# Gated mix of attention and bilinear FFN: scores delayed to share row-tiled stretches, gate folded into FFN and attention values

## Chip, cores and metric

One core of one Trainium2 chip. Times are device microseconds of an execution; the runs with a profile also give the span from the first to the last instruction. A ratio is the mean time of one kernel's runs over that of the other's of the same rounds, so not quite the ratio of the medians quoted. "Same" means within 2%.

Names in the profile lines: PE is TensorE's matmuls, PEld its weight loads, DVE is VectorE, ACT ScalarE, POOL GpSimd; SP only issues transfers here, and SPq is its queue. A line in order of time reads: start in us, length in us, engine, line of the kernel, operation, written tile <- read tiles, count, and in brackets the idle time before it and what ended that.

## The reference

```python
# B=1, S=2048, D=512, 32 heads of 16, F=1376, all bf16
g = sigmoid((x * gate_w).sum(-1, keepdims=True))      # one value per token
q, k, v = heads(x @ wqkv)
a = concat(softmax(q @ k.T / 4) @ v) @ wo
b = ((x @ w_gate) * (x @ w_up)) @ w_down
out = g * a + (1 - g) * b
```

## The kernel before

Queries go in 4 chunks of 512, heads in 4 blocks of 8. A score tile is 128 keys x 512 queries of one head; there are 2048. Scores use row tiling (contraction of 16, padded to 32 rows), almost everything else column tiling (four 32-column matmuls side by side). PSUM is full: psS has two slots of 3 and 2 banks for scores that ACT exponentiates, psO one bank for the attention sums, psX two banks that serve the projections, the FFN and those scores whose exponential DVE approximates. Four such DVE tiles are one *entry*.

No engine decides anything at run time. A Python program in the kernel plays the engines through with assumed durations and so fixes each engine's order of instructions; semaphores then make the real engines wait in that order.

```python
    def dma(self, eng, fn, deps=(), stream=None, dur=0.5, lat=2.2):   # a landing is reckoned at 2.2 us
        return self.op(eng, fn, deps, stream, 16, dur, lat)
# ... cut ...
            def drain(un, last):              # u half of the FFN: plain copy out of PSUM
                        ev_u[n] = un.free = P.op(
                            "dve", lambda v: v.tensor_copy(usb[0:w, n % 2, :], un.bank[0:w, :]), deps, **EV)
# ... cut: down projection, one bank, multiplied with (1 - g) on the way out
                    ev_b[t] = un.free = P.op("dve",
                        lambda v: v.tensor_scalar(bsb[:, t % 5, :], un.bank, omg[:, t : t + 1], None, ALU.mult), ...)
# ... cut: output projection, another bank, combined: out = g * bank + bsb
                o_comb[t] = b_use[t] = P.op("dve",
                    lambda v: v.scalar_tensor_tensor(
                        dst, bank, gval[:, t : t + 1], bsb[:, t % 5, :], ALU.mult, ALU.add), ...)
# ... cut: Q tiles of a head block reach their padded rows by eight transfers issued by SP
                            o = P.dma("sp", lambda e, r0=r0, p=p: e.dma_start(
                                    QX[r0 : r0 + 16, p, b, :], Qst[r0 : r0 + 16, s, :]), ...)
# ... cut: the order of the fills
        fl.append((20, mk_gate(20)))          # the gate, at position 20 (of 512)
        for b in range(1, NB):
            n0 = 32 * b
            fl.append((n0 - 14, mk_q(b, 0, n0 - 14)))      # Q of block 1 at position 18
```

The softmax here doesn't subtract the row's maximum and nothing guards it: scores larger than these inputs give would overflow.

## Time and profile before

| | before |
|---|---|
| time, median of the runs beside the change | 772.52 us (768.78 to 776.87) |
| profiled span | 765.2 us |
| ACT busy | 97% |
| score tiles on ACT / on DVE | 1624 / 424 (106 entries) |
| mean granted TensorE clock | 0.985 |

The last row is read so: the records know only full and half clock, so 2 x (1 - 0.985) x 765 = 23 us were at half. The lines stand in the prediction. Stretch columns are length, then busy us and (count) of PE, PEld, DVE, ACT, POOL, then granted clock, DMA share, GB/s.

### The profile page before, as it was taken

How to read it: one execution, taken by the hardware profiler on the slowest of the kernel's cores; microseconds unless marked ns; L12 is line 12 of the kernel's file. 1: busy time of each engine (PE TensorE's matmuls, PEld its weight loads, DVE VectorE, ACT ScalarE, POOL GpSimd, SP SyncE). 2: the span in 40 equal slices, each digit the busy share in tenths (PEclk: the TensorE clock that was granted, in tenths of full speed). 3: DMA queues.
4: the chain of work that ended last, by engine and by line, in shares of the span. 5: the costliest groups of instructions: out<-in, count | busy, mean ns of one | idle time of the engine just before them, and what ended most of it. 6: DMA issues, size and time to landing. Idle time of an engine off the chain costs nothing.

```text
span 765.2 us, 20615 instructions
## 1 busy us (share of the span) xinstructions
PE 716.2 (94%) x8934; PEld 216.6 (28%) x8934; DVE 665.0 (87%) x1084; ACT 740.9 (97%) x656; POOL 65.6 (9%) x73
## 2 busy tenths in 40 slices
PE   9997899999999999899999989899999999999987
PEld 3332222222222222222222222222232222222234
DVE  3339999899998789999989799989879899999795
ACT  6999999999999999999999999999999999999994
POOL 8940000000000000000000000000000000000000
PEclk9999999999999999989999999989999999999999
DMA  8900000000000100001001000100001101010000
GB/s 169 284 16 10 20 10 24 16 24 16 9 23 9 45 23 9 23 8 31 9 23 36 16 24 9 29 10 6 26 9 30 37 9 30 2 30 9 22 22 34
DMA packets 32880, 22.80 MB, mean 30 GB/s; under 512 B 20468, under 2 KB 27572, under 8 KB 32788
## 3 DMA queue, kind: packets, MB, share of 16 engines
q1 hardware_dynamic: 31476, 20.42, 10.2%
q8 instruction: 70, 1.15, 0.6%
q0 software_dynamic: 256, 0.79, 0.5%
q10 hardware_dynamic: 1056, 0.26, 0.2%
q14 instruction: 22, 0.18, 0.1%
HBM read 11.24 MB, written 2.35 MB: 18 GB/s over the span
## 4 chain that ended last, share of the span: by engine, by line
PE 41%; ACT 33%; DVE 18%; issue 6%; SPq 1%; DMA 1%; DVEq 0%; ACTq 0%
ACT PT L1423 33%; PE psX L368 14%; PE psS L854 12%; PE psO L1069 11%; DVE SC L997 7%; DVE SC L970 5%; PE psX L950 2%; DVE wk L970 2%; PE psO L1079 1%; SPq L1129 1%; DVE usb L630 1%; PE psX L1079 1%; DMA den<-oraw 1%; DVE hT L643 1%; DVE oraw L1122 1%
## 5 line engine op out<-in xcount | busy, mean ns | idle before, releaser
L1423 ACT ACTIVATE PT<-psS 128x1536 bf16<-128x1536 f32 (+1 forms) x646 | 733.2, 1361 | 7.8 <-PE psS L854 3.8
L854 PE MATMUL psS<-QX,KT 32*128 32x512 bf16 x1624 | 256.4, 388 | 32.4 <-ACT PT L1423 29.9
L970 DVE TENSOR_SCALAR SC<-psX 128x512 int16<-128x512 f32 x304 | 203.8, 683 | 22.8 <-PE psX L950 22.4
L997 DVE TENSOR_SCALAR SC<-SC 128x2048 int16<-128x2048 int16 x304 | 205.4, 694 | 2.5 <-PE psO L1069 0.2
L950 PE MATMUL psX<-QX,KT 32*128 32x512 bf16 x424 | 159.6, 386 | 1.6 <-DVE SC L970 0.8
L1069 PE MATMUL psO<-PT,VV 128*32 128x512 bf16 x1566 | 147.1, 390 | 0.7 <-DVE oraw L1122 0.7
L854 PEld LDWEIGHTS psS<-QX,KT 32*128 32x128 bf16 x1624 | 62.2, 91 | 281.7 <-ACT PT L1423 233.0
L1069 PE MATMUL psO<-SC,VD 128*32 128x512 bf16 x1108 | 104.0, 387 | 4.1 <-DVE SC L997 3.3
L970 DVE TENSOR_SCALAR wk<-psX 128x512 int16<-128x512 f32 x120 | 80.7, 683 | 11.8 <-PE psX L950 11.8
L1182 POOL TENSOR_TENSOR OT<-onum,rb 128x512 bf16<-128x512 f32 x16 | 21.7, 1356 | 680.2 <-DMA rb<-rscr 680.2
L997 DVE TENSOR_SCALAR SC<-wk 128x2048 int16<-128x2048 int16 x90 | 62.8, 717 | 0.6
L1069 PEld LDWEIGHTS psO<-PT,VV 128*32 128x32 bf16 x1566 | 37.8, 95 | 64.5 <-issue 55.8
L368 PE MATMUL psX<-wd,hT 128*32 128x512 bf16 (+1 forms) x704 | 52.6, 381 | 0.2 <-DVE wk L970 0.2
L368 PE MATMUL psX<-xT,wu 128*32 128x512 bf16 x688 | 52.0, 394 | 0.2 <-DVE SC L970 0.2
L368 PE MATMUL psX<-xT,wg 128*32 128x512 bf16 x688 | 50.9, 388 | 0.3 <-DVE wk L970 0.3
L950 PEld LDWEIGHTS psX<-QX,KT 32*128 32x128 bf16 x424 | 37.6, 91 | 21.3 <-DVE SC L970 6.0
L1069 PE MATMUL psO<-SC,VV 128*32 128x512 bf16 x408 | 41.2, 390 | 1.6 <-DVE oraw L1122 1.5
L1069 PEld LDWEIGHTS psO<-SC,VD 128*32 128x32 bf16 x1108 | 27.3, 95 | 47.8 <-DVE SC L997 22.2
L643 DVE TENSOR_TENSOR hT<-psX,usb 128x512 bf16<-128x512 f32 (+1 forms) x44 | 30.1, 684 | 4.0 <-PE psX L368 4.0
L630 DVE CAST usb<-psX 128x512 bf16<-128x512 f32 (+1 forms) x44 | 30.1, 683 | 3.9 <-PE psX L368 3.7
L368 PEld LDWEIGHTS psX<-xT,wu 128*32 128x32 bf16 x688 | 15.2, 97 | 23.0 <-issue 10.3
L368 PEld LDWEIGHTS psX<-xT,wg 128*32 128x32 bf16 x688 | 15.3, 95 | 22.0 <-issue 9.4
(108 smaller groups left out, 351.8 us busy)
## 6 DMA issues: line engine op xcount, KB each, us to landing
rb<-rscr SPq DMA_DIRECT2D x16, 256.0 KB
onum<-oraw SPq DMA_DIRECT2D x124, 32.0 KB, 2.0
QX<-Qst SPq DMA_DIRECT2D x120, 16.0 KB, 1.8
out_dram<-ost SPq DMA_DIRECT2D x12, 128.0 KB, 1.7
wu<-in_B_w_up_dram SPq DMA_DIRECT2D x1, 1376.0 KB, 7.3
wg<-in_B_w_gate_dram SPq DMA_DIRECT2D x1, 1376.0 KB, 10.1
wd<-in_B_w_down_dram SPq DMA_DIRECT2D x1, 1280.0 KB, 12.7
SC<-in_A_x_dram SPq DMA_DIRECT2D x4, 128.0 KB, 3.5
```

The costliest lines, as they stand in the source:

```text
L368: r = pe.matmul(dst_[j : j + 32, :], lhs[:, j : j + 32], rhs, start=s0, stop=s1, tile_position=(0, j), skip_group_check=True,)
L630: "dve", lambda v: v.tensor_copy(usb[0:w, n % 2, :], un.bank[0:w, :]), deps, **EV
L643: lambda v: v.tensor_tensor(hT[0:w, f, :], un.bank[0:w, :], usb[0:w, n % 2, :], ALU.mult),
L854: q = pe.matmul(bank_ap(sl, k_), KT[32 * j : 32 * j + 32, b, kt * 128 : (kt + 1) * 128], QX[32 * j : 32 * j + 32, p, b, :], start=True, st ...
L950: lambda pe: pe.matmul(bank, KT[32 * j : 32 * j + 32, b, kt * 128 : (kt + 1) * 128], QX[32 * j : 32 * j + 32, p, b, :], start=True, stop=True,
L970: lambda v: v.tensor_scalar(i2b(nb)[:, j, :], bank, _LO, _HI, ALU.max, ALU.min),
L997: lambda v: v.tensor_scalar(dstt, src, 0.5, _BASE + _OFF[k], ALU.mult, ALU.add),
L1069: r = pe.matmul(psO[r_, :], vcol(m, kt, k_, j), pj, start=first, stop=last, tile_position=(0, 32 * j), skip_group_check=True)
L1079: r = pe.matmul(psO[r_, 256 * hf : 256 * hf + 256] if w < 2 else psD[r_, 0:256], vcol(m, kt, k_, j, hf) if w < 2 else ones[:, k_, 16 - 16 ...
L1122: o_ev[m] = P.op("dve", lambda v: v.tensor_copy(oraw[:, s, :], psO[:]), deps, **EV)
L1182: lambda g: g.tensor_tensor(OT[:, c % 2, b, :], onum[:], rb[:], ALU.mult),
L1423: lambda a: a.activation(cell_ap(cells[0], n).rearrange("p a b -> p (a b)"), bank_ap(sl, 0, n), ACT.Exp, scale=_LN2 / _OCT,),
```

## The change

Its intent: hand TensorE fewer changes of tiling mode (scores wait so that both slots fall into one row-tiled stretch) and DVE less evacuation. The factor 1-g goes into the u half of the FFN, g into the reciprocal that normalizes attention. Then down and output projection can add up in one bank and leave by one plain copy, for chunks 0 to 2. For that the gate is needed in two other layouts: as a row along tokens for all partitions (omgB), and laid out as the softmax sums are (gC). They are made by a trip through HBM. The FFN's work also gets fixed places, chunk by chunk (the list FFN).

```diff
-    D_IDLE = 0.9
-    SLK = 0.15
+    D_IDLE = 1.5
+    SLK = 0.2
+    STAY = 0.25
-    FFN_FROM, FFN_TO = 60.0, 490.0
+    FFN = [(64, 160, 164, 5), (184, 270, 275, 5), (295, 385, 395, 4), (412, 478, 480, 5)]
+    gsc = nc.dram_tensor("gscr", [2, S], F32, kind="Internal").ap()
 ... gate: values to HBM, turned from [token in tile, tile] to token order
+                        for i, src_ in enumerate([gval, omg]):
+                            o = P.dma("sp", lambda e, i=i, src_=src_: e.dma_start(
+                                    gsc[i].rearrange("(t p) -> p t", p=128), src_[:], allow_slow_non_contiguous=True),
+                                [ogate["g"]], "dgs", lat=4.0)
+                        for i in range(8):                      # back, as gC
+                            o1 = P.dma("sp", ... gC[32 * j : 32 * j + 32, :, 16 * p : 16 * p + 16], ... , [o], "dgc")
+                        ogate["c"] = o1
+                        ld_omg(0, [o])                          # back, as omgB, chunk 0; later chunks likewise
 ... FFN
-                            "dve", lambda v: v.tensor_copy(usb[0:w, n % 2, :], un.bank[0:w, :]), deps, **EV
+                            lambda v: v.tensor_tensor(usb[0:w, n % 2, :], un.bank[0:w, :], omgB[0:w, :], ALU.mult),
 ... attention
+                        lambda v: v.tensor_tensor(rec[:, s, 0:w_], rec[:, s, 0:w_], gC[:, c, 0:w_], ALU.mult),
 ... down and output projection in one bank (mk_dw for mk_d and mk_wo, chunks 0 to 2)
+            return Unit(due, chain(FT + NB, mm), deps, drain)
-        fl.append((20, mk_gate(20)))
+        fl.append((16, mk_gate(16)))
 ... TensorE's order
+                hold = t + cost + 0.6 <= need_s() - SLK        # was: cost + 0.49, and for fills only
+            if s and P.mode == "s" and t < s_ready <= t + STAY:  # stay row-tiled, put a DVE score in between
 ... cut: column values picked by pressure, bookkeeping
```

More of the change, by code (lines that the diff above doesn't have):

```diff
@@ L216, in _build @@
         usb = sb("usb", [128, 2, 512], BF16)
-        bsb = sb("bsb", [128, 5, D], BF16)
+        bsb = sb("bsb", [128, 4, D], BF16)
+        omgB = sb("omgB", [128, 512], F32)
+        gC = sb("gC", [128, NCH, 32], F32)
         ost = sb("ost", [128, 2, D], BF16)
@@ L573, in mk_v, with ld_omg @@
             return Unit(due, chain(KD, mm), lambda: [d_wv, ev_x[t]], drain)
-        ogate = {}
+        ogate, o_omg = {}, {}
+        def ld_omg(c, deps):
+            o_omg[c] = P.dma(
+                "sp",
+                lambda e: e.dma_start(omgB[:], bass.AP(gsc.tensor, gsc.offset + S + 512 * c, [[0, 128], [1, 512]])),
+                deps,
+                "domg",
+            )
         def mk_gate(due):
@@ L606, in make @@
                         )
+                        for i, src_ in enumerate([gval, omg]):
+                            o = P.dma(
+                                "sp",
+                                lambda e, i=i, src_=src_: e.dma_start(
+                                    gsc[i].rearrange("(t p) -> p t", p=128), src_[:], allow_slow_non_contiguous=True
+                                ),
+                                [ogate["g"]],
+                                "dgs",
+                                lat=4.0,
+                            )
+                        for i in range(8):
+                            p, j = i % 2, i // 2
+                            o1 = P.dma(
+                                "sp",
+                                lambda e, p=p, j=j: e.dma_start(
+                                    gC[32 * j : 32 * j + 32, :, 16 * p : 16 * p + 16],
+                                    bass.AP(gsc.tensor, gsc.offset, [[16, 32], [512, NCH], [1, 16]]),
+                                ),
+                                [o],
+                                "dgc",
+                            )
+                        ogate["c"] = o1
+                        ld_omg(0, [o])
                     dve_push(3, [e1], make)
@@ L625, in drain @@
                 if which == "u":
-                    deps = [last, u_free.get(n - 2)]
+                    deps = [last, u_free.get(n - 2), o_omg[c]]
                     def make():
                         ev_u[n] = un.free = P.op(
-                            "dve", lambda v: v.tensor_copy(usb[0:w, n % 2, :], un.bank[0:w, :]), deps, **EV
-                        )
+                            "dve",
+                            lambda v: v.tensor_tensor(usb[0:w, n % 2, :], un.bank[0:w, :], omgB[0:w, :], ALU.mult),
+                            deps,
+                            **EV,
+                        )
+                        if f == FT - 1 and c < NCH - 1:
+                            ld_omg(c + 1, [un.free])
                     dve_push(2, deps, make)
@@ L652, in deps @@
                 if which == "u":
+                    r.append(o_omg[c])
                     if n >= 2:
@@ L674, in drain @@
                     h_use[c] = last
-                deps = [last, ogate["g"], b_use.get(t - 5)]
+                deps = [last]
                 def make():
-                    ev_b[t] = un.free = P.op(
-                        "dve",
-                        lambda v: v.tensor_scalar(bsb[:, t % 5, :], un.bank, omg[:, t : t + 1], None, ALU.mult),
-                        deps,
-                        dur=0.65,
-                        lat=0.1,
-                    )
+                    ev_b[t] = un.free = P.op("dve", lambda v: v.tensor_copy(bsb[:, tt, :], un.bank), deps, **EV)
                 dve_push(2, deps, make)
@@ L690, in deps @@
                 r = [d_wd] + [ev_h[c, f] for f in range(FT)]
-                if t >= 5:
-                    r.append(b_use[t - 5])
                 return r
@@ L706, in make @@
                     lambda v: v.scalar_tensor_tensor(
-                        dst, bank, gval[:, t : t + 1], bsb[:, t % 5, :], ALU.mult, ALU.add
+                        dst, bank, gval[:, t : t + 1], bsb[:, t % 4, :], ALU.mult, ALU.add
                     ),
@@ L722, in combine, with mk_dw, mm @@
             dve_push(2, deps, make)
-        def mk_wo(c, tt, due):
+        def mk_dw(c, tt, due):
             t = 4 * c + tt
-            def mm(pe, bk, b, s0, s1):
+            def mm(pe, bk, i, s0, s1):
+                if i < FT:
+                    w = FW[i]
+                    return cmm(pe, bk, hT[0:w, i, tt * 128 : (tt + 1) * 128], wd[0:w, i, :], s0, s1)
+                b = i - FT
                 return cmm(pe, bk, OT[:, c % 2, b, tt * 128 : (tt + 1) * 128], wo[:, b, :], s0, s1)
@@ L731, in drain, with make @@
                 if tt == 3:
-                    ot_use[c] = last
-                combine(t, un.bank, last, un)
+                    ot_use[c] = h_use[c] = last
+                deps = [last, o_out.get(t - 2)]
+                def make():
+                    o_comb[t] = un.free = P.op("dve", lambda v: v.tensor_copy(ost[:, t % 2, :], un.bank), deps, **EV)
+                    o_out[t] = P.dma(
+                        "sp",
+                        lambda e: e.dma_start(out2[t * 128 : (t + 1) * 128, :], ost[:, t % 2, :]),
+                        [o_comb[t]],
+                        f"dout{t % 2}",
+                    )
+                dve_push(2, deps, make)
             def deps():
-                r = [d_wo, ev_b[t]] + [o_mult[c, b] for b in range(NB)]
+                r = [d_wd, d_wo] + [ev_h[c, f] for f in range(FT)] + [o_mult[c, b] for b in range(NB)]
                 if t >= 2:
@@ L739, in deps @@
                 return r
-            return Unit(due, chain(NB, mm), deps, drain)
+            return Unit(due, chain(FT + NB, mm), deps, drain)
         def grp(m):
@@ L1158, in make @@
                 r = P.op("dve", lambda v: v.reciprocal(rec[:, s, 0:w_], den[:, s, 0:w_]), dd + [norm_ops.get(("scr", blk - 2))], dur=0.25)
+                if c < NCH - 1:
+                    r = P.op(
+                        "dve",
+                        lambda v: v.tensor_tensor(rec[:, s, 0:w_], rec[:, s, 0:w_], gC[:, c, 0:w_], ALU.mult),
+                        [r, ogate["c"]],
+                    )
                 norm_ops["rec", blk] = r
@@ L1205, in _build @@
                 fl.append((n0, mk_q(b, c, n0)))
-        n_ffn = NCH * (2 * FT + 4)
-        a0, a1 = FFN_FROM, FFN_TO
-        q = 0
-        for c in range(NCH):
+        for c, (a0, a1, ad, dd) in enumerate(FFN):
             for f in range(FT):
-                for w in "ug":
-                    du = a0 + (a1 - a0) * q / n_ffn
+                for i, w in enumerate("ug"):
+                    du = a0 + (a1 - a0) * (2 * f + i) / (2 * FT)
                     fl.append((du, mk_ug(c, f, w, du)))
-                    q += 1
             for tt in range(4):
-                du = a0 + (a1 - a0) * q / n_ffn
-                fl.append((du, mk_d(c, tt, du)))
-                q += 1
-        for c in range(NCH - 1):
-            fl += [(128 * (c + 1) + 8 + 3 * tt, mk_wo(c, tt, 128 * (c + 1) + 8 + 3 * tt)) for tt in range(4)]
+                du = ad + dd * tt
+                fl.append((du, (mk_dw if c < NCH - 1 else mk_d)(c, tt, du)))
         fl.sort(key=lambda x: x[0])
@@ L1290, in need_s, with d_bank_ok, ride @@
             return sp["x"].t0 + sp["n"] * 0.4267 + 0.064 if sp["x"] else 1e9
+        def d_bank_ok(t):
+            return pick_fill(t + 0.5) is None or any(isinstance(x["u"], Unit) for x in xs)
+        def ride(busy):
+            t = P.t["pe"]
+            xi = x_get(t)
+            if xi is not None and d_bank_ok(t):
+                j = d_can(t, busy)
+                if j is not None:
+                    do_d(j, xi, j in busy)
         def step_pe():
@@ L1295, in step_pe @@
             s_ready = s[0] if s else 1e9
-            hold = False
-            if s and s_ready <= t + 0.01 and spans and P.mode == "c":
-                fs = [u for u in active if u.pos < len(u.mms)]
-                hold = fs and fs[0].mode == "c" and t + fs[0].cost + 0.49 <= need_s() - SLK and need_s() < 1e8
-            if s and s_ready <= t + 0.01 and not hold:
-                busy = do_s(t)
-                xi = x_get(P.t["pe"])
-                if xi is not None and (
-                    pick_fill(P.t["pe"] + 0.5) is None or any(isinstance(x["u"], Unit) for x in xs)
-                ):
-                    j = d_can(P.t["pe"], busy)
-                    if j is not None:
-                        do_d(j, xi, j in busy)
-                return True
             m = st["pvg"]
@@ L1323, in step_pe @@
             fs = [u for u in active if u.pos < len(u.mms)]
+            hold = False
+            if s and s_ready <= t + 0.01 and spans and P.mode == "c" and need_s() < 1e8:
+                cost = MM if pvs else fs[0].cost if fs and fs[0].mode == "c" else 1e9
+                hold = t + cost + 0.6 <= need_s() - SLK
+            if s and s_ready <= t + 0.01 and not hold:
+                busy = do_s(t)
+                ride(busy)
+                return True
+            if s and P.mode == "s" and t < s_ready <= t + STAY:
+                xi = x_get(t)
+                if xi is not None and d_bank_ok(t) and t + MM <= s_ready + 0.07:
+                    j = d_can(t, set())
+                    if j is not None:
+                        do_d(j, xi, True)
+                        return True
+                P.t["pe"] = s_ready
+                return True
             slack = 1e9
@@ L1358, in step_pe @@
             nr = sum(q_[1] is None for q_ in pvs)
-            if pvs and not hold and (not fs or len(tails) or nr >= RP or len(pvs) - nr >= DP):
+            press = sum(q_[1] is None for q_ in p_ring)
+            if pvs and not hold and (not fs or len(tails) or press >= RP or len(pvs) - nr >= DP):
                 pick = "pv"
@@ L1363, in step_pe @@
             if pick == "pv":
-                it = next((q_ for q_ in pvs if (q_[1] is not None) == (nr < RP)), pvs[0])
+                it = next((q_ for q_ in pvs if (q_[1] is not None) == (press < RP)), pvs[0])
                 p_ring.remove(it)
```

## The prediction

> **What bounds the kernel now.** I read the page's engine summary first, then the costliest groups, then busy time in six stretches of 100 us, and last the order of time around single events.
>
> ```profile
> PE 716.2 (94%) x8934; PEld 216.6 (28%) x8934; DVE 665.0 (87%) x1084; ACT 740.9 (97%) x656; POOL 65.6 (9%) x73
> ```
>
> ACT, at 97% of a span of 765.2 us, is the first suspect. What it does is one thing:
>
> ```profile
> L1423 ACT ACTIVATE PT<-psS 128x1536 bf16<-128x1536 f32 (+1 forms) x646 | 733.2, 1361 | 7.8 <-PE psS L854 3.8
> L854 PE MATMUL psS<-QX,KT 32*128 32x512 bf16 x1624 | 256.4, 388 | 32.4 <-ACT PT L1423 29.9
> L970 DVE TENSOR_SCALAR SC<-psX 128x512 int16<-128x512 f32 x304 | 203.8, 683 | 22.8 <-PE psX L950 22.4
> L997 DVE TENSOR_SCALAR SC<-SC 128x2048 int16<-128x2048 int16 x304 | 205.4, 694 | 2.5 <-PE psO L1069 0.2
> L950 PE MATMUL psX<-QX,KT 32*128 32x512 bf16 x424 | 159.6, 386 | 1.6 <-DVE SC L970 0.8
> ```
>
> There are 32 heads x 4 query chunks x 16 key tiles = 2048 score tiles of 128x512. ACT exponentiates 1624 of them (L854 writes them into the slots of three and two banks), at 733.2 / 1624 = 0.4515 us each. The other 424 (L950) go to DVE, four at a time. I call four such tiles an entry: 106 entries now. An entry takes 4 x 0.4515 = 1.81 us off ACT and costs DVE its two TENSOR_SCALAR passes: the L970 and L997 groups together (203.8 + 80.7 + 205.4 + 62.8 + 20.5 us, the forms on the third buffer wk included) are 573 us, or 5.4 us per entry. So the end is set by ACT, and how far ACT's list can be shortened is set by how many entries DVE can be fed. DVE time buys ACT time at 5.4 to 1.81, three to one.
>
> The stretches of the steady part (columns: length, then busy us and count of PE, PEld, DVE, ACT, POOL):
>
> ```profile
> 100.00:200.00 100.00, 93.66 (x1135) 27.27 (x1134) 92.73 (x150) 99.72 (x89) 2.83 (x2) 1.00 0.06 15
> 200.00:300.00 100.00, 94.40 (x1184) 27.62 (x1185) 88.80 (x143) 99.64 (x90) 2.63 (x2) 1.00 0.08 21
> 300.00:400.00 100.00, 93.97 (x1108) 27.02 (x1104) 95.58 (x158) 97.66 (x87) 3.10 (x2) 0.97 0.08 20
> 400.00:500.00 100.00, 94.96 (x1179) 27.16 (x1179) 89.47 (x146) 99.19 (x89) 3.81 (x3) 0.98 0.08 22
> 500.00:600.00 100.00, 96.10 (x1154) 27.32 (x1150) 87.70 (x142) 98.09 (x87) 2.81 (x2) 0.97 0.07 19
> 600.00:700.00 100.00, 93.73 (x1098) 27.14 (x1098) 97.69 (x160) 99.90 (x89) 2.66 (x2) 1.00 0.07 18
> ```
>
> ACT is busy 594 of 600 us, so in the steady part there are only 6 us of ACT waiting to win. DVE is busy 552 of 600: 48 us are idle, most in the stretches with the most projection and FFN matmuls. The waits say what DVE lacks there: 22.4 us on PE for L970 with one buffer and 11.8 us with the other. DVE waits for scores that TensorE issues late or that find no free psX bank.
>
> TensorE's 94% needs a second look, as the record of a matmul (about 0.39 us) is longer than its turn. I took the order of time:
>
> ```profile
> 301.74 0.10 PEld L854 LDWEIGHTS psS<-QX,KT 32*128 32x128 bf16 x3 [0.42 <-ACT PT L1423]
> 301.75 0.39 PE L854 MATMUL psS<-QX,KT 32*128 32x512 bf16 x3
> ...
> 302.28 0.40 PE L1069 MATMUL psO<-PT,VV 128*32 128x512 bf16 x4
> 302.61 0.09 PEld L854 LDWEIGHTS psS<-QX,KT 32*128 32x128 bf16 x2 [0.23 <-ACT PT L1423]
> 302.61 0.39 PE L854 MATMUL psS<-QX,KT 32*128 32x512 bf16 x2
> 302.62 0.09 PEld L950 LDWEIGHTS psX<-QX,KT 32*128 32x128 bf16 x1
> ...
> 302.93 0.10 PEld L1069 LDWEIGHTS psO<-PT,VV 128*32 128x32 bf16 x4 [0.23 <-issue]
> ```
>
> Scores are row-tiled (32 rows), everything else is column-tiled (32 columns). Four column matmuls side by side repeat every 0.2135 us, but from a group at 302.28 to scores is 0.33 us and from the scores at 302.61 back to columns 0.32 us. Each switch of mode thus costs 0.11 us. Counting runs of row-tiled matmuls over the trace gives 658, of which 529 lie in 100 to 700. Two switches each: 529 x 0.22 = 119 us. The same 600 us hold 1288 column groups (275 us) and 529 row turns (113 us). Together 507, so about 93 us are true waiting. TensorE is well loaded, not full.
>
> **What the Trainium skill says.** TensorEngine Tiling (Array Packing), section Key Properties, says that changing the tiling mode drains TensorE, unlike moving between tiles of one mode. The 0.11 us per switch agrees. TensorE: Matmul & The Clock Gate, Part 1, says that a window of 3.4 us with little activity halves the clock. The trace agrees: after 480 to 483 us, with 1.51 us of PE busy in 3.00, this follows:
>
> ```profile
> 483.10:486.30 3.20, 3.15 (x26) 0.80 (x30) 2.05 (x5) 2.39 (x3) 0.00 (x0) 0.50 0.18 41
> 506.90:513.60 6.70, 6.70 (x53) 1.23 (x50) 4.54 (x8) 4.91 (x5) 0.00 (x0) 0.50 0.10 21
> ```
>
> There are four such half-clock stretches, about 20 us in all, and ACT loses about 5 us in them: less work on TensorE is not free of risk. VectorE: DVE Perf Modes, section "Why PSUM operands drop a tier", says that an fp32 PSUM operand leaves DVE at 1x. The trace agrees: cast 683 ns, tensor by tensor 684 ns from PSUM.
>
> **The change part by part.** (1) Gate folding, chunks 0 to 2. Twelve output tiles lose their bsb multiply (L681, mean 741 ns): 8.9 us. Twelve combines (L706, 745 ns) become plain copies (683 ns as the casts): 0.7 us. The usb cast becomes a multiply with an fp32 row in SBUF: by the hT multiply's 684 ns, plus 0. Twelve small multiplies of 128x32 are added: by the 128x16 tensor-scalar's 174 ns about 0.19 each, 2.2 us. DVE net: 8.9 + 0.7 - 2.2 = 7.4 us free, 1.4 entries, 2.5 us of ACT. (2) Down and output projection in one bank: the same matmuls, but twelve evacuations and twelve bank turns fewer. A psX bank is then held for 15 groups, 3.2 us, rather than 11 and 4. Small gain, within part 4. (3) Gate moved from position 20 to 16, about 6 us earlier. DVE now stands 4.99 us behind the gate's exponential, at 44.8 to 49.7 us, just as DVE entries begin. Earlier, that wait falls before them. Half of it counted: 2.5 us of DVE. The new transfers (values to HBM and back, about a dozen issues, plus three reloads of the gate row) run long before the FFN of that chunk. Landings of such rows take 1.7 to 2.0 us now: zero on the path. (4) The new order. Staying row-tiled when the other slot is about to free, more readiness to issue a DVE score alone (allowed DVE backlog 0.9 to 1.5), and column values counted by pressure, save row runs. If 529 falls by 15%, TensorE gets 80 x 0.22 = 18 us back. What that is worth is DVE kept fed: I let the steady part go from 92% to 95.5% busy, as its better stretches show (95.6 and 97.7), 3.5% of 600 = 21 us. This is the largest term and the one I chose.
>
> Sum on DVE: 7.4 + 2.5 + 21 = 31 us, at 5.4 us per entry 5.7, so about 6 entries: 106 to 112. ACT then has 24 tiles fewer, 24 x 0.4515 = 10.8 us, all on the path. Profiled span 765.2 - 10.8 = 754.4, a ratio of 0.986. Of the median 773.45 us that makes 762.5 us.
>
> **The rivals.** (A) DVE stays unfed: free bank turns and the two-buffer limits, not TensorE's turns, pace the entries. Then only parts 1 and 3 count: 9.9 / 5.4 = 1.8 entries, 3.3 us, 770 us. For it: TensorE already has 93 us of waiting and DVE idles all the same. Against: the stretch at 97.69% runs with the same banks. (B) Scores issued later make ACT wait, or a TensorE kept idle in row mode falls to half clock. Now scores for the two-bank slot are issued a median of 1.02 us, for the three-bank slot 0.82 us, before the previous exponential ends. Losing 2% of ACT's 600 us is 12 us, 774 us. Against: the change raises its planned margin (0.49 + 0.15 to 0.6 + 0.2 us). (C) All works: DVE at 98% from 100 to 700 gives 36 + 9.9 = 46 us, 8.5 entries, 15 us, and 3 us fewer ACT waits. 18 us, 755 us. Past that DVE is the bound.
>
> **Range and chances.** Between B and a little beyond C: 748 to 773 us. Two per cent faster is 758 us, and needs about 8.5 entries or fewer throttled stretches besides; I give it 0.25. Slower by two per cent needs ACT starved on a scale that the larger margin speaks against: 0.06. Within two per cent: 0.69.
>
> **What would show it.** Right: L854's score count falls from 1624 to about 1600 and L950's rises from 424 to about 448; fewer row-tiled runs than 658; DVE above 94% in 100 to 700 with ACT still at 99%; no bsb for twelve tiles. Wrong: L950 near 430 (A), or ACT under 98% in 100 to 700 with waits on L854 or more half-clock stretches (B). A count above 456 would mean that I undervalued TensorE's turns.

## More of the kernel before

```profile
24.00:100.00 76.00, 68.81 (x850) 21.15 (x848) 54.34 (x90) 75.04 (x68) 23.49 (x22) 0.98 0.23 72
```

ACT is busy 75 of 76 us there.

## The result, and the profile after

796.74 us median (791.33 to 798.94, 4 runs) against 772.52: ratio 1.0301, 95% interval 1.0225 to 1.0378. Slower, and outside the predicted range of 748 to 773 us.

| | before | after |
|---|---|---|
| profiled span | 765.2 us | 796.0 us |
| ACT busy in the exponential groups | 733.2 us | 735.2 us |
| ACT idle before them | 7.8 us | 36.8 us |
| score tiles on ACT / DVE | 1624 / 424 | 1624 / 424 |
| row-tiled runs on TensorE (my count) | 658 | 627 |
| mean granted clock | 0.985 | 0.954 |

First the engine summary, the granted clock in 40 slices, and the groups that answer to those shown of before:

```profile
PE 737.2 (93%) x8898; PEld 219.1 (28%) x8898; DVE 660.7 (83%) x1084; ACT 743.0 (93%) x656; POOL 66.3 (8%) x73
PEclk9997558999999999999999999999999999999999
L1491 ACT ACTIVATE PT<-psS 128x1536 bf16<-128x1536 f32 (+1 forms) x646 | 735.2, 1362 | 36.8 <-PE psS L905 29.0
L1001 PE MATMUL psX<-QX,KT 32*128 32x512 bf16 x424 | 159.1, 397 | 19.7 <-DMA QX<-Qst 14.6
```

ACT does the same work in the same time and waits 29.0 us longer; that is all but 2 us of the 30.8 us. The DVE share did not grow by one tile. The clock falls to half in slices 5 and 6. The stretches say where the waiting is:

```profile
24.00:100.00 76.00, 55.34 (x619) 15.10 (x607) 34.05 (x56) 53.12 (x48) 22.57 (x21) 0.77 0.24 65
100.00:200.00 100.00, 95.19 (x983) 24.90 (x983) 82.40 (x133) 91.38 (x81) 2.98 (x2) 0.85 0.06 15
200.00:300.00 100.00, 95.00 (x1118) 27.59 (x1114) 97.77 (x163) 99.47 (x89) 5.03 (x3) 1.00 0.09 23
```

Against the kernel before, ACT is short of 21.9 us in the first stretch and of 8.3 us in the second: 30 us, all before 200 us. From 200 to 700 us it is busy 496.8 of 500, against 494.5 before. The steady part is not worse.

What ACT waits for is a chain that starts on SP's queue. The order of time there, around the gate:

```profile
54.32 0.43 SPq L624 DMA_DIRECT2D gscr<-gval  x1
54.80 0.94 SPq L624 DMA_DIRECT2D gscr<-omg  x1
73.67 3.65 SPq L635 DMA_DIRECT2D gC<-gscr  x8
77.36 0.43 SPq L585 DMA_DIRECT2D omgB<-gscr  x1
77.83 4.97 SPq L511 DMA_DIRECT2D QX<-Qst  x8
```

The two stores are 2 x 2048 elements of 4 bytes, each to a place of its own. SP issues them at 54.3 to 55.7 us, and then waits 17.9 us for them, because the reload of gC needs what they wrote. The transfers of Q for head block 1 stand behind that wait, with which they have nothing to do. TensorE and ACT in that time:

```profile
68.85 0.61 PE L905 MATMUL psS<-QX,KT 32*128 32x512 bf16 x3 [0.37 <-ACT PT L1491]
84.10 0.60 PE L1001 MATMUL psX<-QX,KT 32*128 32x512 bf16 x2 [14.65 <-DMA QX<-Qst]
```
```profile
66.43 4.62 ACT L1491 ACTIVATE PT<-psS 128x1024 bf16<-128x1024 f32 x4 [3.38 <-remote]
86.26 1.02 ACT L1491 ACTIVATE PT<-psS 128x1024 bf16<-128x1024 f32 x1 [15.21 <-PE psS L905]
```

TensorE stands 14.65 us for QX, ACT 15.21 us. The 3.38 us before that fall on ACT and DVE at once, with TensorE waiting for ACT, while the small writes are under way. In the DMA records a fetch of instructions (16 KB) took 5.1 us there; the like one in the kernel before took 1.3 us. It may be the cause, but no run tests it, and its record (64.7 to 69.8 us) covers only part of the standing (63.0 to 66.4 us). And then the clock:

```profile
68.10:126.10 58.00, 42.76 (x282) 7.83 (x278) 31.54 (x51) 33.91 (x29) 1.27 (x1) 0.50 0.08 20
```

For 58 us TensorE has half clock: from just after that 3.4 us pause, through the gap, and for 42 us beyond its end at 84 us. ACT loses 8 us in waits of 0.4 to 1.8 us between 87 and 126 us.

The part that was counted well: the twelve new copies and the twelve small multiplies:

```profile
L776 DVE CAST ost<-psX 128x512 bf16<-128x512 f32 x12 | 8.2, 682 | 0.0
L1213 DVE TENSOR_TENSOR rec<-rec,gC 128x32 f32<-128x32 f32 x12 | 2.3, 192 | 0.4
```

### The profile page after: what moved, and what is told of

Same layout as the page of the kernel before. It is cut to its first block, busy times and chain, and to the rows that moved or that the text cites. A ratio compares the mean times of both kernels' runs of the same rounds, so it can differ in the third digit from the quotient of the medians.

```text
span 796.0 us, 20513 instructions
## 1 busy us (share of the span) xinstructions
PE 737.2 (93%) x8898; PEld 219.1 (28%) x8898; DVE 660.7 (83%) x1084; ACT 743.0 (93%) x656; POOL 66.3 (8%) x73
## 4 chain that ended last, share of the span: by engine, by line
ACT 35%; PE 27%; DVE 21%; issue 8%; DMA 4%; SPq 2%; POOL 2%; POOLq 0%; DVEq 0%; ACTq 0%
ACT PT L1491 35%; DVE SC L1048 8%; PE psO L1120 8%; PE psX L372 8%; PE psS L905 8%; DVE SC L1021 5%; DVE wk L1021 3%; DMA gscr<-omg 2%; PE psX L1001 2%; SPq L1180 1%; DVE usb L668 1%; DVE hT L685 1%; DMA den<-oraw 1%; PE psS L1279 1%; DVE oraw L1173 1%
## 5 line engine op out<-in xcount | busy, mean ns | idle before, releaser
L1491 ACT ACTIVATE PT<-psS 128x1536 bf16<-128x1536 f32 (+1 forms) x646 | 735.2, 1362 | 36.8 <-PE psS L905 29.0
L905 PE MATMUL psS<-QX,KT 32*128 32x512 bf16 x1624 | 261.1, 396 | 24.6 <-ACT PT L1491 19.9
L1048 DVE TENSOR_SCALAR SC<-SC 128x2048 int16<-128x2048 int16 x304 | 209.9, 708 | 2.1
L1120 PE MATMUL psO<-PT,VV 128*32 128x512 bf16 x1562 | 156.6, 398 | 1.0 <-POOL VV L567 1.0
L1120 PE MATMUL psO<-SC,VD 128*32 128x512 bf16 x1120 | 109.7, 403 | 3.9 <-DVE SC L1048 3.6
L1048 DVE TENSOR_SCALAR SC<-wk 128x2048 int16<-128x2048 int16 x90 | 59.3, 683 | 0.3
L372 PE MATMUL psX<-wd,hT 128*32 128x512 bf16 (+1 forms) x704 | 56.2, 382 | 0.1
L1120 PEld LDWEIGHTS psO<-PT,VV 128*32 128x32 bf16 x1562 | 40.5, 97 | 56.8 <-issue 42.5
L372 PE MATMUL psX<-xT,wg 128*32 128x512 bf16 x688 | 55.3, 389 | 0.7 <-DVE SC L1021 0.7
L668 DVE TENSOR_TENSOR usb<-psX,omgB 128x512 bf16<-128x512 f32 (+1 forms) x44 | 30.0, 682 | 2.0 <-PE psX L372 1.8
L1173 DVE COPY oraw<-psO 128x512 f32<-128x512 f32 x31 | 21.2, 683 | 4.2 <-PE psO L1120 4.0
## 6 DMA issues: line engine op xcount, KB each, us to landing
wg<-in_B_w_gate_dram SPq DMA_DIRECT2D x1, 1376.0 KB, 10.4
```

What stands on the lines that cost most here:

```text
L372: r = pe.matmul(dst_[j : j + 32, :], lhs[:, j : j + 32], rhs, start=s0, stop=s1, tile_position=(0, j), skip_group_check=True,)
L668: lambda v: v.tensor_tensor(usb[0:w, n % 2, :], un.bank[0:w, :], omgB[0:w, :], ALU.mult),
L905: q = pe.matmul(bank_ap(sl, k_), KT[32 * j : 32 * j + 32, b, kt * 128 : (kt + 1) * 128], QX[32 * j : 32 * j + 32, p, b, :], start=True, st ...
L1048: lambda v: v.tensor_scalar(dstt, src, 0.5, _BASE + _OFF[k], ALU.mult, ALU.add),
L1120: r = pe.matmul(psO[r_, :], vcol(m, kt, k_, j), pj, start=first, stop=last, tile_position=(0, 32 * j), skip_group_check=True)
L1173: o_ev[m] = P.op("dve", lambda v: v.tensor_copy(oraw[:, s, :], psO[:]), deps, **EV)
```

## The experiments

Theory A: the 4-byte store and SP's wait for it hold up Q, and half clock follows. Rivals: (B) the new order is slower in itself; (C) the flood of small writes takes the DMA engines, wherever it is issued. Each ratio below is against runs of the kernel before in the same rounds on the same chip. The batches (e1 to e4, e5 to e8, e9 to e12, e13 to e16, e17 and e18) ran on different chips or at different times, so across batches the ratios are compared and not the medians.

| run | kernel | median us | ratio (95%) |
|---|---|---|---|
| e1_rows | change, gate stored as 32 rows of 512 B | 777.05 | 1.011 (1.006 to 1.017) |
| e2_pool | change, store and reloads issued by GpSimd | 780.21 | 1.015 (1.009 to 1.020) |
| e3_gate20 | change, gate at position 20 | 789.63 | 1.026 (1.021 to 1.030) |
| e4_order | before + new order only | 772.70 | 1.004 (0.998 to 1.011) |
| e5_store_wait | before + store and waiting reloads | 784.36 | 1.018 (1.014 to 1.022) |
| e6_store_nowait | before + store, nobody waits | 781.69 | 1.015 (1.010 to 1.020) |
| e7_warm | change + 66 idle matmuls in the gap | 790.34 | 1.026 (1.022 to 1.030) |
| e8_rows_oldorder | folding with rows, old order rules | 786.96 | 1.022 (1.018 to 1.026) |
| e9_gate16 | before, gate at 16 | 774.71 | 1.006 (1.002 to 1.010) |
| e10_rows_lat | e8, rb reckoned at 4.5 us | 776.19 | 1.009 (1.004 to 1.014) |
| e11_tuned_rows | e1, numbers searched | 775.02 | 1.007 (1.003 to 1.010) |
| e12_tuned_before | before, numbers searched | 777.06 | 1.010 (1.006 to 1.014) |
| e13_before_keep | before + repeated scores | 770.64 | 1.001 (0.998 to 1.003) |
| e14_rows_keep | e1 + repeated scores | 770.07 | 1.000 (0.998 to 1.003) |
| e15_tbefore_keep | e12 + repeated scores | 765.88 | 0.996 (0.992 to 0.999) |
| e16_trows_keep | e11 + repeated scores | 771.11 | 1.002 (0.999 to 1.004) |
| e17_best_before | second search, no folding, repeats | 762.93 | 0.988 (0.984 to 0.992) |
| e18_best_rows | second search, folding, repeats | 773.58 | 1.003 (0.998 to 1.007) |

### The store (e1 to e7, e9)

**e1_rows.** The gate values are made bf16, turned by one matmul with the identity, and stored in one transfer of long rows:

```diff
-                        for i, src_ in enumerate([gval, omg]):
-                            o = P.dma("sp", ... gsc[i].rearrange("(t p) -> p t", p=128), src_[:] ...)
+                        P.op("dve", lambda v: v.tensor_copy(gpk[:, 0:16], gval[:]), ...)
+                        e5 = P.op("dve", lambda v: v.tensor_copy(gpk[:, 16:32], omg[:]), ...)
+                        tr = P.op("pe", lambda pe: pe.matmul(un.bank[0:32, 0:128], gpk[:], ident[:], ...), [e5, o_id], ...)
+                        un.free = P.op("dve", lambda v: v.tensor_copy(gtr[:], un.bank[0:32, 0:128]), [tr], dur=0.2)
+                        o = P.dma("sp", lambda e: e.dma_start(gsc.rearrange("i (t p) -> (i t) p", p=128), gtr[:]), [un.free], "dgs")
```

> The changed kernel, but the gate values are turned on TensorE first, so that they reach HBM as 32 rows of 512 bytes in one transfer and not as 4096 elements of 4 bytes in two; everything after that is as in the change. Theory A (the slow landing of the 4-byte store, 17.9 us of waiting in SP's queue, holds up the Q tiles of the second head block, TensorE stands 15 us and then runs 58 us at half clock): the wait falls below 4 us, the 15 us gap of TensorE and ACT and the long half-clock stretch go, time 762 to 772 us, ratio to before 0.985 to 1.005. Rival B (the new order itself is slower: fewer banks for DVE, later scores): the time stays above 785 us although the gap is gone.

The order of time on SP's queue in this run:

```profile
53.89 0.43 SPq L643 DMA_DIRECT2D gscr<-gtr  x1
55.40 3.71 SPq L651 DMA_DIRECT2D gC<-gscr  x8
59.16 0.43 SPq L587 DMA_DIRECT2D omgB<-gscr  x1
59.63 6.07 SPq L513 DMA_DIRECT2D QX<-Qst  x8
```

The reload follows its store by 1.5 us (1.1 us of it waiting) where it was 18.9, Q leaves 18 us earlier, and the 15 us gap is gone. The time is 1.9 points of ratio better. So the 4-byte store with its wait stands for two thirds of the loss; this run does not part the two. But 777 us lies between the ranges of A and B, and the run is still 1.1% slower than before: something else is in it.

**e2_pool and e3_gate20.**

```diff
 e2: the two stores, the eight reloads and the first omgB
-                                "sp",
+                                "pool",
 e3:
-        fl.append((16, mk_gate(16)))
+        fl.append((20, mk_gate(20)))
```

> The changed kernel with the same 4-byte store, but store, the eight reloads and the first gate row are issued by GpSimd and not by SP. Theory A in the form that SP's queue is what is blocked: the Q tiles of the second block are issued in time, no 15 us gap, time 762 to 775 us. Rival C (the flood of 4096 small writes itself takes the transfer engines, so that other transfers and the fetch of instructions wait wherever the store is issued): a gap of 3 us or more of all engines at once stays near the store, and the time stays above 780 us.

> The changed kernel with one number undone: the gate at position 20 as before, so after the Q projection of the second head block (18) and not ahead of it. Theory A: the store still lands 18 us late and SP still waits, but the Q tiles of the second block are already on their way, so most of the 15 us gap goes: 770 to 782 us, as the order worked out for this position is itself about 10 us longer (103 DVE entries for 106). Rival B: above 790 us.

e2 took 780.21 us, outside theory A's range and just inside C's. With SP free, ACT still has gaps of 2.8 and 6.4 us near the store, and GpSimd waits 18.2 us for the landing:

```profile
53.35 5.96 SPq L511 DMA_DIRECT2D QX<-Qst  x8
70.34 0.57 POOL L635 DMA_DIRECT2D gC<-gscr  x1 [18.19 <-DMA gscr<-omg]
72.80 0.61 PE L1001 MATMUL psX<-QX,KT 32*128 32x512 bf16 x2 [5.70 <-DMA QX<-Qst]
```

SP issued Q from 53.35 us on, on its own queue, and TensorE still waited for it until 72.80 us; such a transfer lands 1.8 us after its issue in the kernel before. So the small writes hold Q up from another queue too. Issuing from GpSimd saves 1.5 of the 3.0 points. The traces suggest why: Q no longer stands behind the reloads, and TensorE goes on 2.5 us after these begin, in the change 10.4 us after (84.10 against 73.67). Whether e2 is slower than e1 is not clear of noise. e3 missed what was expected. The gap is gone, but the order worked out for this position has three entries fewer and had another 7 us gap at its end. It doesn't isolate the store: inconclusive.

**e5, e6 and e9: the store alone, in the kernel before.** e5 adds the stores and the reloads (unused), e6 the stores only, e9 is the control with nothing but the gate's position.

> The kernel before, with the gate at position 16 and with the 4-byte store and the eight reloads that wait for it on SP's queue; what they bring is not used, everything else is as before. Theory A (store and wait suffice for two thirds of the loss): a gap of TensorE and ACT of 10 us or more between 55 and 90 us, a long half-clock stretch behind it, time 785 to 797 us, ratio 1.02 to 1.035. Rival B (the loss needs the new order or the folding): within 1% of before, below 778 us.

> As the run with store and wait, but without the reloads: the two 4-byte stores are issued by SP and nothing waits for them. If it is SP's wait for the landing that holds the Q tiles back: they are issued 18 us earlier, no gap above 5 us, time 768 to 780 us. If the queue itself (later transfers stand behind 4096 small writes, fetches of instructions too) is what costs: as slow as with the wait, 783 us or more.

> Control: the kernel before with the gate at position 16 and nothing else. Its order is exactly that of the run with the unwaited store, less the two stores. If the store is what costs there: within 0.6% of before, 766 to 775 us, against 781.7 with the store. If the moved gate costs: 778 us or more, and the store is cleared.

e5 has the gap (ACT 12.7 us), though at 784.36 us it is a hair below its range: no long tail of half clock followed (17 us of it). e6, between its two ranges, is the surprise. Nobody waits, Q is issued right after the stores, and it is slow all the same:

```profile
46.52 0.39 SPq L612 DMA_DIRECT2D gscr<-gval  x1
46.95 0.95 SPq L612 DMA_DIRECT2D gscr<-omg  x1
47.95 7.58 SPq L509 DMA_DIRECT2D QX<-Qst  x8
66.79 0.58 PE L962 MATMUL psX<-QX,KT 32*128 32x512 bf16 x1 [5.92 <-DMA QX<-Qst]
```

TensorE still waited 5.9 us for that QX, as it landed only with the last of the small writes. e6 and e9 have the same order: 781.69 against 774.71 us, so 0.9 points are the store's alone without any wait on SP. The gate's move costs 0.6 points by itself. What the wait adds to the store, e5 against e6, is 0.3 points and not clear of noise; the two orders differ a little besides (107 entries in e5, 106 in e6).

**e7_warm.** 66 full-width matmuls into the bank about to be overwritten, placed where TensorE stands:

```diff
+            if (c, b) == (0, 1) and not dst.get("warmed"):          # once; cut
+                P.op("pe", lambda pe: [pe.matmul(bank, xT[:, 0, 0:128], xT[:, 0, 0:512], start=True, stop=True) for _ in range(66)][-1], ...)
```

> The changed kernel, and in the place where TensorE stands for 15 us 66 matmuls of full width into the bank it is about to fill (their results are overwritten): 14 us of work that only keep the clock up. Theory A with two parts (15 us of standing, then about 10 us of ACT waits in the 58 us of half clock): the standing remains, the long half-clock stretch is cut to under 10 us, time 783 to 790 us, against 796.7. If half clock was harmless there, 795 us or more.

The standing stays (ACT 15.15 us), the 58 us of half clock become stretches of 10.2 us and less, and the time is 790.34 us, just above the range expected. Against the change that is 0.4 points of ratio less (3 us; 6 us by the medians), and the intervals overlap: the clock after the gap costs a few us at most, well below the 10 that I had expected, and perhaps nothing.

### Order and folding (e4, e8, e10)

> The kernel before with only the new ordering rules of TensorE (holding, staying row-tiled, backlog 1.5), no folding, no new transfers. Theory A: the order costs nothing by itself: within 1% of before, 765 to 778 us, 104 DVE entries for 106. Rival B: slower by 2% or more, with ACT waiting for scores from 100 us on.

> The changed kernel with the gate values turned into rows and with the ordering rules of before (no staying in row mode, backlog 0.9, margin 0.15): the folding alone, the fourth corner beside before, the order alone (ratio 1.0042) and both (1.0111). The order worked out for it is 6.5 us longer than that of before. If the folding with its longer bank turns is what the last 1% comes from: 775 to 785 us. If the order is: within 0.5% of before, 767 to 774 us.

The edits are the halves of the diff: e4 has only TensorE's rules and the three numbers, e8 all but those, with the store as rows. The order alone is within 1%. The folding alone is 2.2% slower, though with both it is 1.1%. In e8 TensorE stands in its fixed order behind a projection whose normalized values have not come; PE waited 7.2 us for OT at one place, and ACT:

```profile
603.95 1.02 ACT L1488 ACTIVATE PT<-psS 128x1024 bf16<-128x1024 f32 x1 [4.30 <-PE psS L920]
762.67 2.37 ACT L1488 ACTIVATE PT<-psS 128x1024 bf16<-128x1024 f32 x2 [7.24 <-PE psS L920]
```

The ordering program reckons 2.2 us for the landing of rb; from issue to use it took 3.7 to 6.2 us in the kernel before. e10 changes this number:

```diff
-                d = P.dma("sp", lambda e: e.dma_start(rb[:], bc), [w] + prv, "drb")
+                d = P.dma("sp", lambda e: e.dma_start(rb[:], bc), [w] + prv, "drb", lat=4.5)
```

> Folding with rows and the ordering rules of before (786.96 us), with one number changed: the program that fixes the order reckons 4.5 us rather than 2.2 for the landing of the reciprocal row rb (the traces show 3.6 to 6.2). Theory D (the folding's rest is TensorE standing in its fixed order behind a projection whose normalized values have not landed: 4.3 and 7.2 us of ACT waiting): both waits fall below 1.5 us and the time to 768 to 778 us. If not: above 783 us.

It came to 776.19 us, as expected, and the 7.24 us gap is gone; the other shrank only to 2.3 us, with another of 2.7 us behind it, so not quite below 1.5. The new order also has 108 entries in place of 106, so the run does not test the number alone. It is still 0.9% slower than before, about where e1 is (1.1%).

### Half clock (e11 to e18)

e11 and e12 took the ordering numbers from a search over some 700 orders worked out without the chip.

> The folding with rows, with the numbers of the ordering rules searched anew (700 tries of the ordering program, no chip) and rb reckoned at 3.8 us: the order worked out ends 2.2 us earlier than that of the run with rows (777.05). If the rest of the loss is a matter of the order alone: 762 to 774 us. If the folding costs in any order: 775 us or more.

> The kernel before, no folding, with its five ordering numbers searched in the same way: 108 DVE entries for 106, the order worked out ends 4.2 us earlier. Expected 0.2 to 0.8% faster than before, 764 to 769 us, if the chip follows the order; no difference or slower if waits that the order does not reckon with (half clock, landings) decide.

Neither gained. e11, at 775.02 us, lies a hair inside the range for a folding that costs in any order. e12 missed its range and took its other branch, waits that the order does not reckon with: it has two entries more and an order that ends 4 us sooner, and is 1.0% slower than before. Its profile shows where:

```profile
24.00:100.00 76.00, 73.68 (x715) 19.56 (x711) 49.25 (x77) 64.12 (x56) 23.77 (x22) 0.73 0.21 68
```

The clock is 0.73, and ACT misses 11 us against the kernel before. So I cut the 14 traces that I had into windows of 3.41 us in step with the changes of clock, and took the share of each window in which a matmul was streaming (512 columns at the granted clock). 82 windows at full clock were followed by half clock: median share 0.45, none above 0.59. For 2760 that stayed at full clock the median is 0.76, and 95% are above 0.56. Half clock ended only after windows of 0.71 or more, counted at half speed. So half clock follows thin use of TensorE, but not every thin window. A recount of the same traces gives: below a share of 0.39, 25 of 25 windows were followed by half clock; from 0.39 to 0.59, 55 of 275; above, none of 2563. Whether it *causes* the waits is what e13 to e16 ask: the same orders, instruction for instruction, but where the ordering program counts less than 0.60 of 3.4 us streamed, scores are computed again, the same values into the same bank.

```diff
+            more = dict(n=0)
-                for k_, ((m, kt), j) in enumerate(un):
+                for k_, ((m, kt), j) in list(enumerate(un)) * (1 + more["n"]):
+        # after the order is fixed: where TensorE would stream less than 0.6 of 3.4 us
+            short = 0.6 * 3.4 - sum(d for a_, d in P.stream if x <= a_ < x + 3.4)
+            while short > 0 and any(sp["more"]["n"] < 2 for sp in inside):
+                sp = min(inside, key=lambda sp: sp["more"]["n"]); sp["more"]["n"] += 1; short -= 0.2135
```

> The kernel before in the very same order, but where that order would leave TensorE streaming less than 0.60 of 3.4 us, scores are computed a second or third time into the same bank with the same values (some 150 extra score turns of 0.21 us). Theory H (half clock follows a window of 3.4 us with less than about half of it streamed, and the waits of ACT follow half clock): half-clock stretches fall from 20 us to under 7 us, ACT gaps near them from 5.8 to under 3 us; 0 to 0.6% faster, 766 to 771 us. Rival (half clock is only a sign of waits that are there anyway): the same or slower by the extra work.

> The folding with rows and the new order (777.05 us), order unchanged, with the same repeats. Theory H: half-clock stretches before the end of ACT's work fall from 37.5 us to under 12 us, ACT gaps near them from 10.2 to under 5 us, time 767 to 773 us, which is before's. Rival: above 775 us.

> The kernel before with the five searched numbers (777.06 us, 108 entries, 61 us of half clock, 18 us of ACT gaps near it), order unchanged, with the repeats. Theory H: half clock below 15 us, gaps near it below 6 us, time 760 to 768 us, so faster than before. Rival: above 774 us.

> The folding with rows and searched numbers (775.02 us, 44 us of half clock), order unchanged, with the repeats. Theory H: half clock below 15 us, time 763 to 770 us. Rival: above 773 us.

The granted clock rises to 0.996, 0.997, 1.000 and 0.999. With that, e14 (rows and the new order) goes from 777.05 to 770.07 us, ratio 1.000: the open third of the loss is gone. e15 goes from 777.06 to 765.88 us. The same stretch of e15 as shown of e12:

```profile
24.00:100.00 76.00, 73.62 (x917) 22.55 (x913) 56.38 (x91) 73.50 (x66) 23.63 (x22) 1.00 0.21 65
```

More matmuls than in e12 (917 for 715), and ACT has 9.4 us more done; over the whole run ACT's idle time before its exponentials falls from 22.1 to 6.9 us. That is the causal test: the order is the same but for the repeats, which by themselves only add work, and with them the half clock goes. For e14 the two lines are (e1 first):

```profile
L1507 ACT ACTIVATE PT<-psS 128x1536 bf16<-128x1536 f32 (+1 forms) x646 | 734.4, 1355 | 15.9 <-PE psS L921 11.4
L1512 ACT ACTIVATE PT<-psS 128x1536 bf16<-128x1536 f32 (+1 forms) x646 | 734.4, 1324 | 9.3 <-PE psS L926 7.5
```

e16 gains less than hoped (771.11 us; the range ended at 770). For the kernel before itself the repeats are worth nothing (e13): it has little half clock, and though gaps near it fall from 5.8 to 2.7 us, the time does not; where that is lost is not shown. e14 and e13 ran in the same rounds with nearly the same clock: folding and new order 770.07 us, neither 770.64 us.

The last two take the best order of a second search, one without and one with the folding, both with repeats (share 0.57).

> No folding: the best order of a second search (109 DVE entries, its order ends 6.3 us before that of the kernel before) with the repeats of scores where TensorE would stream less than 0.57 of 3.4 us. If half clock is what kept searched orders from paying: no half-clock stretch, 760 to 766 us, ratio 0.988 to 0.996. If not: 768 us or more.

> The folding with rows, the best order of the second search (107 entries, its order ends 3.0 us before that of the run with rows) with the repeats. If the folding is worth its 7.4 us of DVE as 1.4 entries: faster than the best order without it, below 762 us. If, as the counts of entries say, the freed DVE time does not become entries: 764 to 770 us, at or behind the run without folding.

e17 is the fastest kernel: 762.93 us, 1.2% faster than before, with 109 entries; by the 2% rule it is "same", but its interval, 0.984 to 0.992, excludes 1. e18, with the folding, is at 773.58 us, above both of its ranges. It has 107 entries and one half-clock stretch of 13.7 us left, at the gate, so the pair does not measure the folding purely. It shows no gain from it.

## Why the prediction was wrong

**The bound.** Right: ACT sets the end, its work was the same 646 instructions, and every us lost is a us of ACT waiting.

**Part 1, DVE operations.** Right term by term: the copies took 682 ns (predicted 683), the small multiplies 192 ns each (0.19), the u multiply 682 ns against 683 for the cast. As a sum it is less clear: DVE was busy 665.0 us before and 660.7 after, 4.3 us for the 7.4 counted.

**Part 3, the transfers. This step failed first.** The text put them at "zero on the path", because landings take 1.7 to 2.0 us. Those landings were of rows of 1 to 2 KB; rows of 64 bytes (rscr) held SP for 1.4 us each. The new store writes 4096 elements of 4 bytes: 17.9 us of waiting on SP, with Q behind it, and small writes that delay other transfers even where nobody waits (e6) or where another engine issues them (e2). I looked at when the gate's *consumers* need the values and not at what stands behind the store in the same in-order queue. Size: 1.9 of the 3.0 points (e1 against the change), of which 3 to 6 us may be the clock after the gap (e7, not clear of noise). The same part's moved gate did shorten DVE's wait before it, from 5.0 to 0.9 us; alone, in e9, it made the kernel 0.6 points slower.

**Part 4, the new order. This failed too.** I let DVE fill to 95.5% and had six more entries. There are none: 106 before and after. Row-tiled runs fell by 5% (658 to 627; 529 to 500 in the steady part), not by the 15% assumed, and DVE in 200 to 700 us went from 459 to 457 us busy. The number of entries is a property of the order, and I had estimated it from idle time. The ordering program's own count, with one assumed duration changed at a time in the kernel before, shows how loose that link is: with the sixteen (1-g) multiplies made nearly free it gives 105 entries (0.05 us each; 107 with 0.1 us), with free mode switches 113, with evacuations a third shorter 118. The best order that the searches found, e17's, has 109. The program needs no chip: run as it stands, it gives 106 entries for both kernels and an end only 2.2 us earlier for the change, so this term could have been read before predicting. It also reckons 4.0 us for the landing of the store; with 18 there, its end for the change moves from 749.1 to 762.7 us. So it was the supply of entries that failed; the trade of three to one was not put to the test. (A slip without effect: 529 x 0.22 is 116 us and not 119, so the true waiting is 96 us and not 93.)

**The rivals.** B named half clock as a danger and set it at 774 us. In kind it was right: the last 1.1 points go when the clock is kept up (e14). But B had it come from staying in row mode; the runs show it after thinly used stretches of 3.4 us whatever thins them, and the longest stretch began after the 3.4 us pause and held through the gap that the transfers made. No rival held a transfer queue.

**Left open.** Whether the folding, well ordered and at full clock, is worth anything: with the new order and the repeats it equals the kernel before with the repeats (e14, e13), and e18 is behind e17 with another order. Why the folding alone needs the new order to be bearable (e8) is shown only in part by its two waits. The cause of the 3.4 us pause of ACT and DVE is open. What SP's wait costs beyond the writes themselves is not settled either: 1.5 points by e2 against the change, 0.3 by e5 against e6.

## What to carry to other kernels

Before adding a transfer, ask which unrelated transfers stand behind it and behind its wait in the issuing engine's queue, and which others will be under way beside it. Count its pieces, not its bytes: turn small data on TensorE and store long rows. In a kernel whose engines follow a fixed order, idle time on one engine is not supply for another; count what the order really places. And where TensorE is thinly used beside a busy ACT, look at the granted clock: repeating harmless matmuls made two slower orders 1.1 and 1.4% faster (ratios of e14 to e1 and of e15 to e12).

## What the Trainium skill lacked or had wrong

- DMA: Bandwidth & Descriptors, section Specifications, gives 512 bytes as the least size for line rate and says that below it there is a read-modify-write. Small pieces are slow: 2 x 2048 elements of 4 bytes to HBM kept a waiting SP queue for 17.9 us; the values, rounded to bf16, as 32 rows of 512 bytes for 1.1 us. That the pieces are read before they are written no run shows. What the page lacks is a figure for the other transfers beside such a store: TensorE waited 5.9 us for tiles issued behind it on the same queue (e6), and 5.7 us where another engine had issued the store (e2).
- TensorE: Matmul & The Clock Gate, Part 1, speaks of an idle window of about 3.4 us before the clock halves. Here full idleness isn't needed, and the page gives no share of use: windows with a median of 45% streaming, and up to 58%, were followed by half clock, below 39% all of them. Nor does a busy window end it at once: the change had 58 us of half clock, 42 us of them after the gap had ended, eleven windows in a row with 76 to 86% streaming among them. The page's section Why this matters for your kernels advises to warm up with matmuls before one measures; in mid-kernel more matmuls helped as well: mean clock 0.961 to 1.000 (e12 to e15).
- TensorEngine Tiling (Array Packing), Key Properties, says that a mode switch drains TensorE but gives no duration. In the kernel before it was 0.11 us each way.
